# Every converted weight block written to DRAM in the first chunk, and a higher transfer rate in the planner

## The chip, the cores and the metric

The kernel runs on one core of a Trainium2 chip. The metric is the device time of one execution in microseconds; several executions were timed and the median is given. Six streams of instructions matter here: TensorE (PE, with its weight loads as PEld), VectorE (DVE), ScalarE (ACT), GpSimd (POOL), and SyncE (SP), which issues the DMAs.

## What is computed

Linear attention with random features over 4 batches, 8 heads, 576 tokens and a head size of 64, and then two gated feed-forward layers over the 2304 tokens (512 channels, 1536 hidden). The weights of the two layers come in as 64-bit floats.

```python
def phi(x):
    proj = np.einsum('bhsd,md->bhsm', x, omega)
    h = proj - np.sum(x * x, axis=-1, keepdims=True) / 2.0
    h = h - np.max(h, axis=-1, keepdims=True)
    return np.exp(h) / np.sqrt(m)
q_p, k_p = (phi(q_s), phi(k_s))
kv = np.einsum('bhsm,bhsd->bhmd', k_p, v)
num = np.einsum('bhsm,bhmd->bhsd', q_p, kv)
den = np.einsum('bhsm,bhm->bhs', q_p, np.sum(k_p, axis=2))[..., None] + 1e-06
x = num / den                        # then tokens x 512
g = x @ w_gate
x = (g / (1 + np.exp(-g)) * (x @ w_val)) @ w_out      # layer 0
x = ((x @ w_a) * (x @ w_b)) @ w_out2                  # layer 1
```

## The kernel before

The 2304 tokens are worked in five chunks: two of 512, one of 256, and two of 512 that run together as a pair. Each chunk passes through attention and both layers; the attention of a later chunk runs between the layer matmuls of the one before it. Every matmul of a layer is done as three: each operand is split into a rounded part and a remainder (`wh` and `wl` for weights, `xh`/`xl` and `hh`/`hl` for activations), and L908, L909 and L910 add up high by high, high by low and low by high. `product` (L966) does the same for the pair.

A layer has 36 weight blocks of 128 x 512, so the two have 72. A block that is converted goes through five steps: a DMA of 512 KB into one of four raw buffers (`w64a`, three of them, or `w64b`, L865); two ACT instructions that bring exponent and mantissa into place (L868 into a buffer `w`, L871 in the raw buffer); two DVE instructions that join sign and halves (L874, L877); then the split, ACT for `wh` (L889) and DVE for `wl` (L458). `w` is a ring of four buffers (`w32`), `wh` and `wl` have seven each. `weights` decides with `keep` in which chunk the converted `w` is also written to DRAM (`kept`, L883, 256 KB): blocks of even number in chunk 0, blocks of odd number in chunk 1. A later chunk loads the kept block (L887, 256 KB, and L1028 in the pair) and only splits it. An odd block is therefore converted twice. A buffer `w` comes free when its split is done and its store, where it has one, has landed.

No order is written out by hand. Every operation is recorded with a due time, and `Plan.order` plays the program through with costs of its own: an engine takes, of what is ready by its account, the operation that is due first. The instructions of each engine are then issued in that order, and on the chip each engine keeps to it. For a DMA the planner has one pipe that moves `RATE` MiB in a microsecond; a higher `RATE` makes data ready earlier in its account and lets operations stand earlier in the order.

The features of the later chunks (`features` with `STACKED`) run through a short chain: PE projects into one of two PSUM buffers `ps_p` (L561), ACT copies half of it to `kf` or `qf` (L569), DVE adds the other half (L572), which frees `ps_p` for PE's next L561.

Of the kernel before, what the change touches and what calls it, by code (L numbers as in the profile page):

```python
# [88 lines left out]
class Plan:  # L89
# [11 lines left out]
    SIGNAL = 0.12  # L101
    START = 0.7
    TABLE = 1.4
    RATE = 0.24
    HELD = {DVE: (1.0, 0.05), POOL: (1.0, 0.12)}

    def __init__(self):
# [27 lines left out]
    def order(self):  # L135
# [36 lines left out]
        while True:  # L172
# [51 lines left out]
            if o.size:  # L224
                pipe = max(pipe, t + 1.0) + o.size / self.RATE
                o.end = pipe + 1.2
# [28 lines left out]
def attention_moe_moe(ctx: ExitStack, tc: tile.TileContext, qT, kT, q, k, v, omegaT,  # L255
# [596 lines left out]
    def weights(c, m, i, due):  # L852
# [2 lines left out]
        ahead = AHEAD if c else 0.0  # L855
        parts_of[c, m, i] = (hi, lo)
        w = r_w32.buf()
        keep = i % 2
        if c <= keep:


# [425 lines left out]
```

## Time and profile before

| | |
|---|---|
| median of 3 runs | 1015.7 us (1015.49 to 1016.5) |
| profiled execution | 1016.63 us, of which the span is 1014.8 us |
| PE busy | 994.4 us, 98% of the span |
| DVE busy | 880.8 us, 87% |
| ACT busy | 731.1 us, 72% |
| DMA | 153.12 MB, 151 GB/s on average, about 240 GB/s in the first 300 us |
| granted TensorE clock | 1.00 throughout |

The span is what the profiler saw from the first to the last instruction; about 1.8 us of the execution's time lie around it. PE is busy nearly all the time and the clock is full, so the places to look at are the few microseconds in which PE stands, and what it waits for there. By the stretches of the trace, chunk 0 runs to about 283 us, chunk 1 to about 550 us, and chunk 2 and the pair fill the rest.

### The profile page before, as it was taken

The page shows a single profiled execution, that of the slowest core. Times are in us where ns is not written, and L with a number is a line of the kernel's source. Part 1 is how long each engine was busy: PE and PEld are TensorE (multiplying, and loading weights), DVE is VectorE, ACT ScalarE, POOL GpSimd, SP SyncE. Part 2 cuts the span into 40 slices and gives each one's busy share as a digit, 9 for nine tenths or more (in the row PEclk, how much of TensorE's full clock was granted, in tenths as well). Part 3 has the DMA queues.
Part 4 walks back from the last instruction along what each step waited for, and adds up shares of the span by engine and source line. Part 5 has one row for each costly group of instructions (what it writes and reads, how often), then busy time and mean ns, then how long its engine had stood idle before and what let it go on. Part 6 is the DMA issues. An engine that isn't in the chain of part 4 may idle for free.

```text
span 1014.8 us, 15549 instructions
## 1 busy us (share of the span) xinstructions
PE 994.4 (98%) x5212; PEld 836.8 (82%) x5212; DVE 880.8 (87%) x1697; ACT 731.1 (72%) x1519; POOL 228.3 (22%) x178
## 2 busy tenths in 40 slices
PE   7999999999999999999999999999999999999998
PEld 6878888888888878777778999988888887888886
DVE  5999889999858889999996989799899788989972
ACT  5987988898779998978788988576574645556340
POOL 1232011111204242346544324311020021202000
PEclk9999999999999999999999999999999999999999
DMA  7777787776854657735654555521212211121212
GB/s 248 238 260 237 217 247 238 248 237 218 279 187 133 182 176 236 225 113 176 196 170 130 158 155 163 175 80 42 74 42 63 84 32 52 30 75 42 63 32 83
DMA packets 92399, 153.12 MB, mean 151 GB/s; under 512 B 8736, under 2 KB 41120, under 8 KB 92320
## 3 DMA queue, kind: packets, MB, share of 16 engines
q1 hardware_dynamic: 92240, 152.11, 48.9%
q8 instruction: 41, 0.67, 0.3%
q14 instruction: 38, 0.31, 0.1%
q10 hardware_dynamic: 80, 0.03, 0.0%
HBM read 128.52 MB, written 23.59 MB: 150 GB/s over the span
## 4 chain that ended last, share of the span: by engine, by line
PE 73%; DVE 11%; ACT 7%; DMA 4%; issue 3%; POOL 1%; SPq 0%; DVEq 0%; ACTq 0%; POOLq 0%
PE ps_m L966 13%; PE ps_m L908 9%; PE ps_m L910 9%; PE ps_m L909 9%; PE ps_p L966 8%; PE ps_t L966 8%; PE ps_kv L966 4%; PE ps_kv L640 2%; DVE wl L458 2%; DMA w64a<-w 2%; PE ps_p L586 2%; PE ps_t L735 1%; PE ps_p L561 1%; DVE w64a L874 1%; DVE w L877 1%
## 5 line engine op out<-in xcount | busy, mean ns | idle before, releaser
L458 DVE TENSOR_TENSOR wl<-w,wh 128x512 fp32r<-128x512 f32 x256 | 194.4, 769 | 23.6 <-ACT wh L889 22.9
L908 PE MATMUL ps_m<-xh,wh 128*128 128x512 f32 (+1 forms) x500 | 188.8, 378 | 2.1 <-ACT a L926 1.4
L909 PE MATMUL ps_m<-xl,wh 128*128 128x512 f32 (+1 forms) x500 | 183.4, 367 | 0.2 <-DVE xl L458 0.2
L910 PE MATMUL ps_m<-xh,wl 128*128 128x512 f32 (+1 forms) x500 | 183.2, 366 | 0.1
L889 ACT ACTIVATE wh<-w 128x512 fp32r<-128x512 f32 x224 | 137.8, 631 | 25.5 <-DVE w L877 10.0
L458 POOL TENSOR_TENSOR rs<-xT,rs 64x576 fp32r<-64x576 f32 (+4 forms) x48 | 67.8, 1413 | 232.8 <-ACT rs L546 112.3
L908 PEld LDWEIGHTS ps_m<-xh,wh 128*128 128x128 f32 x500 | 94.8, 190 | 17.6 <-issue 2.4
L910 PEld LDWEIGHTS ps_m<-xh,wl 128*128 128x128 f32 x500 | 94.3, 189 | 16.3 <-DVE wl L458 0.5
L909 PEld LDWEIGHTS ps_m<-xl,wh 128*128 128x128 f32 x500 | 94.6, 189 | 11.2 <-DVE xl L458 0.8
L908 PE MATMUL ps_m<-hh,wh 128*128 128x512 f32 (+1 forms) x252 | 94.8, 376 | 0.0
L910 PE MATMUL ps_m<-hh,wl 128*128 128x512 f32 (+1 forms) x252 | 92.2, 366 | 0.2 <-DVE wl L458 0.2
L909 PE MATMUL ps_m<-hl,wh 128*128 128x512 f32 (+1 forms) x252 | 92.2, 366 | 0.0
L871 ACT ACTIVATE w64a<-w64a 128x512 uint32<-128x512 uint32 x90 | 60.6, 680 | 17.7 <-DMA w64a<-w 17.4
L877 DVE SCALAR_TENSOR_TENSOR w<-w,w64a 128x512 uint32<-128x512 uint32 x90 | 67.0, 749 | 2.8 <-ACT w L868 2.5
L874 DVE SCALAR_TENSOR_TENSOR w64a<-w64a 128x512 uint32<-128x512 uint32 x90 | 64.6, 726 | 3.1 <-ACT w64a L871 3.1
L868 ACT ACTIVATE w<-w64a 128x512 f32<-128x512 f32 x90 | 60.1, 672 | 0.0
L910 PEld LDWEIGHTS ps_m<-hh,wl 128*128 128x128 f32 x252 | 47.6, 189 | 8.7 <-DVE wl L458 0.7
L458 DVE TENSOR_TENSOR hl<-h,hh 128x512 fp32r<-128x512 f32 (+1 forms) x72 | 50.6, 704 | 2.9 <-ACT hh L932 2.2
L908 PEld LDWEIGHTS ps_m<-hh,wh 128*128 128x128 f32 x252 | 47.7, 189 | 6.1
L909 PEld LDWEIGHTS ps_m<-hl,wh 128*128 128x128 f32 x252 | 47.7, 189 | 5.2
L932 ACT ACTIVATE hh<-h 128x512 fp32r<-128x512 f32 (+1 forms) x72 | 40.1, 558 | 14.9 <-DVE h L929 14.7
L929 DVE TENSOR_TENSOR h<-a,ps_m 128x512 f32<-128x512 f32 (+1 forms) x63 | 38.8, 615 | 12.7 <-PE ps_m L910 8.8
(822 smaller groups left out, 2635.4 us busy)
## 6 DMA issues: line engine op xcount, KB each, us to landing
w64a<-w SPq DMA_DIRECT2D x90, 512.0 KB, 4.5
w<-kept SPq DMA_DIRECT2D x180, 256.0 KB, 2.7
kept<-w SPq DMA_DIRECT2D x72, 256.0 KB, 5.0
w64b<-w SPq DMA_DIRECT2D x18, 512.0 KB, 4.8
kt<-k_t SPq DMA_DIRECT2D x16, 320.0 KB, 3.8
vt<-v_t SPq DMA_DIRECT2D x16, 320.0 KB, 4.8
xT<-kT SPq DMA_DIRECT2D x16, 288.0 KB, 3.2
qt<-q_t SPq DMA_DIRECT2D x16, 256.0 KB, 3.4
```

The lines of the kernel that those rows point to most:

```text
L458: eng.tensor_tensor(out=out, in0=a, in1=hi.bitcast(F32), op=ALU.subtract)
L868: on(ACT, act(CW + 50), due - ahead - 10, lambda: nc.scalar.activation(out=w.tile, in_=raw.tile[:, :, 1].bitcast(F32), func=AF.Abs, scale= ...
L871: on(ACT, act(CW + 50), due - ahead - 10, lambda: nc.scalar.activation(out=raw.tile[:, :, 0], in_=raw.tile[:, :, 0], func=AF.Copy, scale=0 ...
L874: on(DVE, dve(CW, True), due - ahead - 9, lambda: nc.vector.scalar_tensor_tensor(out=raw.tile[:, :, 0], in0=raw.tile[:, :, 1], scalar=0x80 ...
L877: on(DVE, dve(CW, True), due - ahead - 9, lambda: nc.vector.scalar_tensor_tensor(out=w.tile.bitcast(U32), in0=w.tile.bitcast(U32), scalar= ...
L889: on(ACT, act(CW), due - ahead - 7, lambda: nc.scalar.activation(out=hi.tile.rearrange("p a c -> p (a c)"), in_=w.tile, func=AF.Copy), rea ...
L908: nc.tensor.matmul(o, lhsT=hi.tile[:, wi], rhs=a, start=first, stop=False)
L909: nc.tensor.matmul(o, lhsT=hi.tile[:, wi], rhs=b, start=False, stop=False)
L910: nc.tensor.matmul(o, lhsT=lo.tile[:, wi], rhs=a, start=False, stop=last)
L929: on(DVE, dve(n), due, lambda a=a, h=h, ps=ps: nc.vector.tensor_tensor(out=h.tile[:, 0:n], in0=a.tile[:, 0:n], in1=ps[1].tile[:, 0:n], op= ...
L932: on(ACT, act(n), due + 2, lambda h=h, hh=hh: nc.scalar.activation(out=hh.tile[:, 0:n], in_=h.tile[:, 0:n], func=AF.Copy), reads=[(h,)], w ...
L966: nc.tensor.matmul(ps.tile, lhsT=flat(a.tile)[:, k], rhs=b.tile, start=first and i == j == 0, stop=last and i == len(w) - 1 and j == 2, sk ...
```

## The change

Two lines. `keep` becomes 0 for every block: all 72 blocks are converted once, in chunk 0, and written to DRAM there; chunk 1 loads all of its blocks from `kept`. And the planner's `RATE` goes from 0.24 to 0.28 MiB/us.

```diff
-    RATE = 0.24
+    RATE = 0.28
...
         w = r_w32.buf()
-        keep = i % 2
+        keep = 0
         if c <= keep:
```

In the built program L865, L868, L871, L874 and L877 stand 72 times each where they stood 108 times; L887 stands 152 times where it stood 116 times; L883 stands 72 times in both. PE has the same instructions in another order.

SP's queue in the middle of layer 0 of chunk 0, before (`w64a` and `w64b` are loads of a raw block, `kept_18` is the store of block 18, and the number behind `w_` is the buffer):

```order
L865 DMA w64a_170<-w 128x1024
L865 DMA w64b_171<-w 128x1024
L883 DMA kept_18_203<-w_174 128x512
L865 DMA w64a_169<-w 128x1024
L883 DMA kept_20_204<-w_172 128x512
L865 DMA w64a_168<-w 128x1024
L865 DMA w64b_171<-w 128x1024
L865 DMA w64a_170<-w 128x1024
```

The same place in the changed program:

```order
L865 DMA w64a_169<-w 128x1024
L865 DMA w64a_170<-w 128x1024
L883 DMA kept_17_211<-w_173 128x512
L883 DMA kept_18_212<-w_174 128x512
L865 DMA w64b_171<-w 128x1024
L865 DMA w64a_168<-w 128x1024
L883 DMA kept_19_213<-w_175 128x512
L883 DMA kept_20_214<-w_172 128x512
```

Loads and stores now come two by two, and every one of the four `w` buffers carries a store.

DVE in layer 1 of chunk 1, ahead of the two L572 that the trace of before has at 485.5 us, before (`wl` is a block's remainder, `hl` that of an activation; `mx`, `top`, `bias`, `nsq` and `s` are small steps of the features):

```order
L874 SCALAR_TENSOR_TENSOR w64a_169<-w64a_169 128x512
L599 SCALAR_TENSOR_TENSOR top_102<-mx_98,nsq_94 128x2
L458 TENSOR_TENSOR wl_186<-w_174,wh_179 128x512
L603 TENSOR_TENSOR bias_106<-nsq_94,top_102 128x2
L458 TENSOR_TENSOR wl_187<-w_172,wh_180 128x512
L877 SCALAR_TENSOR_TENSOR w_175<-w_175,w64a_169 128x512
L458 TENSOR_TENSOR hl_164<-h_141,hh_152 128x512
L530 TENSOR_SCALAR nsq_92<-s_89 128x10
L530 TENSOR_SCALAR nsq_94<-s_90 128x8
L527 TENSOR_REDUCE s_89<-qt_114 128x8
L572 TENSOR_TENSOR qf_115<-qf_115,ps_p_64 128x256
L572 TENSOR_TENSOR qf_115<-qf_115,ps_p_65 128x256
```

The same place in the changed program:

```order
L458 TENSOR_TENSOR wl_189<-w_175,wh_182 128x512
L596 TENSOR_REDUCE mx_98<-kf_82 128x2
L458 TENSOR_TENSOR hl_164<-h_141,hh_152 128x512
L599 SCALAR_TENSOR_TENSOR top_102<-mx_98,nsq_94 128x2
L603 TENSOR_TENSOR bias_106<-nsq_94,top_102 128x2
L530 TENSOR_SCALAR nsq_94<-s_90 128x8
L527 TENSOR_REDUCE s_90<-qt_114 128x8
L572 TENSOR_TENSOR qf_115<-qf_115,ps_p_64 128x256
L572 TENSOR_TENSOR qf_115<-qf_115,ps_p_65 128x256
```

Between the remainder `hl_164` and the two L572 the order is nearly the same; the two conversion steps and two of the `wl` that stood ahead of it are gone or stand elsewhere.

## Rows read from the trace of the kernel before

**Rows 1.** Waits of PE, whole span: who waited, for whom, us, times, longest.
```profile
PE ps_m L586 <- DMA xT<-kT: 4.6, 1, 4.6
PE ps_p L561 <- DVE kf L572: 3.0, 5, 1.1
PE ps_p L561 <- DVE qf L572: 2.4, 2, 1.3
```

**Rows 2.** Busy time by stretch: us, engines (x instructions), granted clock, DMA share, GB/s.
```profile
0.00:60.00 60.00, 52.13 (x305) 43.26 (x306) 46.25 (x135) 44.90 (x123) 13.50 (x21) 1.00 0.79 246
60.00:130.00 70.00, 69.91 (x321) 58.00 (x320) 64.23 (x104) 57.54 (x104) 10.25 (x6) 1.00 0.77 236
130.00:283.00 153.00, 152.75 (x812) 129.85 (x811) 141.65 (x290) 124.32 (x262) 24.10 (x17) 1.00 0.77 242
...
350.00:550.00 200.00, 193.58 (x1023) 157.01 (x1022) 177.74 (x361) 169.49 (x394) 91.83 (x74) 1.00 0.58 179
550.00:1014.80 464.80, 459.04 (x2425) 393.19 (x2423) 400.92 (x716) 273.32 (x522) 73.58 (x48) 1.00 0.28 81
```

**Rows 3.** PE in time, 483.9 to 486.5 us: start, us, instruction, idle before.
```profile
485.96 0.39 PE L561 MATMUL ps_p<-oms,rs 128*128 128x256 f32 x1 [1.30 <-DVE qf L572]
```

**Rows 4.** DVE in time, 481 to 486 us.
```profile
483.28 0.68 DVE L877 SCALAR_TENSOR_TENSOR w<-w,w64a 128x512 uint32<-128x512 uint32 x1
...
484.74 0.69 DVE L527 TENSOR_REDUCE s<-qt 128x8 f32<-128x512 f32 x1
485.48 0.75 DVE L572 TENSOR_TENSOR qf<-qf,ps_p 128x256 f32<-128x256 f32 x2
```

**Rows 5.** Costliest groups, page: shapes, count, busy us, mean ns, idle before.
```profile
L871 ACT ACTIVATE w64a<-w64a 128x512 uint32<-128x512 uint32 x90 | 60.6, 680 | 17.7 <-DMA w64a<-w 17.4
L877 DVE SCALAR_TENSOR_TENSOR w<-w,w64a 128x512 uint32<-128x512 uint32 x90 | 67.0, 749 | 2.8 <-ACT w L868 2.5
L874 DVE SCALAR_TENSOR_TENSOR w64a<-w64a 128x512 uint32<-128x512 uint32 x90 | 64.6, 726 | 3.1 <-ACT w64a L871 3.1
L868 ACT ACTIVATE w<-w64a 128x512 f32<-128x512 f32 x90 | 60.1, 672 | 0.0
```

**Rows 6.** DMA issues, whole span: count, KB each, median us to landing.
```profile
w<-kept SPq DMA_DIRECT2D x180, 256.0 KB, 2.7
kept<-w SPq DMA_DIRECT2D x72, 256.0 KB, 5.0
```

**Rows 7.** DMA traffic and issues from 60 to 130 us.
```profile
DMA packets 7886, 16.55 MB, mean 236 GB/s; under 512 B 631, under 2 KB 3463, under 8 KB 7880
...
w64a<-w SPq DMA_DIRECT2D x17, 512.0 KB, 4.5
kept<-w SPq DMA_DIRECT2D x11, 256.0 KB, 5.2
w64b<-w SPq DMA_DIRECT2D x5, 512.0 KB, 4.6
```

**Rows 8.** Busy time by stretch again, for two stretches with dense traffic.
```profile
135.00:145.00 10.00, 10.00 (x53) 8.51 (x53) 7.78 (x16) 6.39 (x16) 1.32 (x1) 1.00 0.99 310
...
250.00:275.00 25.00, 25.00 (x134) 21.18 (x133) 21.61 (x41) 19.19 (x41) 7.17 (x5) 1.00 0.87 265
```

**Rows 9.** SP's queue in time, 255 to 295 us.
```profile
258.67 0.32 SPq L887 DMA_DIRECT2D w<-kept  x1
...
285.86 0.34 SPq L956 DMA_DIRECT2D outT<-h  x1
```

**Rows 10.** Engines in time, 100.3 to 103 us: one block from conversion to store.
```profile
100.50 0.67 ACT L868 ACTIVATE w<-w64a 128x512 f32<-128x512 f32 x1
...
102.49 0.43 SPq L883 DMA_DIRECT2D kept<-w  x1
```

**Rows 11.** All transfers of kept blocks: shortest, median and longest time to landing.
```profile
DMA to landing us min/median/max: 2.3/2.9/9.0
```

**Rows 12.** Waits of all engines, whole span: ACT for the raw blocks.
```profile
ACT w64a L871 <- DMA w64a<-w: 17.4, 11, 4.1
```

## The prediction, made before the changed kernel ran

> **What bounds the kernel now.** I read the busy shares first: PE 98% of the span at the full clock, DVE 87%, ACT 72%. Then the table of stretches [rows 2], where one subtraction per row gives PE's idle time: 7.9 us in the first 60 us, 0.1 from 60 to 130, 0.2 from 130 to 283, 6.4 from 350 to 550, and 5.8 in the last 465 us. The amount of PE's work does not change, so the change can only move these idle times, or make new ones where there are none now. The list of PE's waits [rows 1] says what they are: at the start one wait of 4.6 us for the first keys, which comes ahead of all weights, and then seven waits of L561, 5.4 us together, for DVE's L572 to free `ps_p`. All seven lie in the second chunk, in the stretch of the 6.4 us. Read one of them in time: PE stands 1.30 us before the L561 at 485.96 [rows 3], because DVE reaches L572 only at 485.48, with a conversion step (L877) and a reduction among the work just ahead of it [rows 4]. DVE is 89% busy there [rows 2]; a step that comes due finds a queue in front of it.
>
> In the first chunk the picture is turned round. PE hardly stands there, but DVE is busy 92 to 93%, ACT 81 to 82%, and the DMA engines 77% at 236 to 242 GB/s [rows 2]. It is fed just in time by four resources at once.
>
> **What the change removes.** 36 conversions in the second chunk. On DVE 36 x (0.749 + 0.726) = 53.1 us, on ACT 36 x (0.672 + 0.680) = 48.7 us [rows 5]. Spread over the 267 us from 283 to 550 that is 0.20 us in every us of DVE: the 89% of the stretch becomes about 69%, and ACT's 85% about 67%. Neither engine is the bound, so the 53 us themselves are worth nothing; what they are worth is the queue ahead of L572. Bounds: nothing, if the planner packs other steps into the gaps and L572 is late again; 6.4 us if all idle time of the stretch goes. At the place shown in the order, two conversion steps and two remainders stood ahead of the L572 that cost 1.30 us, and in the changed program L527 and four small steps are still there. I take 4.5 us, seven tenths of the stretch: the waits of L561 are 5.4 of the 6.4, and most of them are shorter than two conversion steps (1.3 us is the longest, 1.48 us two steps). What would be late next is ACT, whose L569 feeds L572; it is relieved as much.
>
> **What it adds, first the traffic.** The 36 odd blocks are stored in the first chunk: 36 x 256 KB = 9.4 MB more there. In the second chunk 36 loads of 512 KB become 256 KB and 36 stores vanish, 18.9 MB less, at a share of 0.58 that hinders nobody now. The tight place is 60 to 130 us: 22 loads of blocks and 11 stores, 16.55 MB [rows 7]. With 11 more stores (2.9 MB) it is 19.4 MB, 278 GB/s over the same 70 us. Can the engines carry that? The densest 10 us carried 310 GB/s at a share of 0.99, and the densest 25 us 265 GB/s at 0.87 [rows 8]. At 310 the 19.4 MB take 63 us, and nothing is lost; at 265 they take 73.3 us, 3.3 us more than now, all of it on PE, which has no reserve here. 265 is no ceiling, since the share was 0.87, but 310 was held only for 10 us. I take the middle, 1.5 us. From 130 to 283 the stores add as much per us, but here the first load for the second chunk is issued at 258.67 while the first chunk's last output leaves at 285.86 [rows 9]: a lead of 27 us, or some 6.5 MB at 242 GB/s, covers the 5 to 6 MB of stores. I cost it at nothing; without the lead it would be 5.5 MB at 265 GB/s, up to 6 us more where PE waits for blocks. At the start three odd stores (0.8 MB, 3 us of transfer at 265 GB/s) fall between the loads of the first blocks and of the attention: nothing to 3 us, below nothing by 1 if the new order suits the start better; I take 0.5, since the wait that dominates there [rows 1] comes before any store.
>
> The Trainium skill, "DMA: Bandwidth & Descriptors", section Specifications, gives some 358 GB/s as what HBM allows a core, by which the 19.4 MB would take 54 us and the 1.5 us would be zero. The trace doesn't carry this: share 0.77 at 236 GB/s, and 0.99 at 310, both point to a little over 300 GB/s for these transfers [rows 2, 8].
>
> **Then the waits.** Every buffer `w` of the first chunk now also waits for its store. The nearest row: L868 fills one at 100.50, its store is issued at 102.49 [rows 10], and lands 5.2 us later (median of the stretch) [rows 7], so a buffer is held for 7.2 us. Four buffers at one block per 70/22 = 3.2 us leave 12.7 us. With the longest landing seen, 9.0 us [rows 11], it would be 11.0 us: still inside. So I cost the ring at nothing; it decides from a landing of 10.7 us on. The new wait sits on L868, at the head of ACT's queue: behind it stand the evacuations L926 and L932, without which PE's `ps_m` buffers don't come free. SP's queue is moved too: stores stand two by two, each behind the load that the same conversion releases, so no load is held up by them for long; each store adds its 0.43 us of issue [rows 10] on a queue that mostly waits.
>
> By the Trainium skill, same page, section "Anatomy of one DMA", the end of a DMA is reported only once its last byte is confirmed in the target, and HBM is the slowest target. The rows agree: 5.0 us for a store against 2.7 for a load of the same 256 KB [rows 6].
>
> **The rate.** 0.28 MiB/us is 294 GB/s. It costs nothing by itself; it decides how early in the order conversions stand. In the order of the changed program they do stand earlier against PE's work in the first chunk, by about two blocks for much of layer 0, which gives some cover for late transfers. In the later chunks the instructions are the same and their order differs in detail; PE's idle time there (5.8 us) may change by 1 us either way, and I count zero.
>
> **The sum.** -4.5 + 1.5 + 0.5 = -2.5 us on the span of 1014.8 us. The profiled execution took 1016.63 us, 0.9 above the median of 1015.7; against the median the forecast is 1013.2 us.
>
> **The rivals.**
>
> *Same.* The relief is real but L572 is late for another reason: the planner, too, sees the free DVE and sets PE's L561 earlier, so that PE meets the chain as tightly as before. Two of the 6.4 us go, and the first chunk costs 2. For it: L572 comes after L569 on ACT, and PE's order is fixed by a plan that fills gaps. Against it: the wait in [rows 3] has conversion steps directly in its queue. It gives 1015.7.
>
> *Slower.* L868 waits for stores. If traffic at 90% and more makes stores land above 10.7 us, ACT stands at L868 with the evacuations behind it. The nearest row for such a wait is ACT's L871 waiting for its load, 17.4 us in all, in 11 waits among its 108 runs [rows 12], so about 1.6 us each. If it strikes one in six of the 36 newly stored blocks, 6 x 1.6 = 9.6 us on ACT, nearly all on PE between 60 and 130 us, where there is no lead: say 8. With -4.5 and +2 that is +5.5, or 1021.2 us. For it: four resources are tight at the same time. Against it: the ring has 12.7 us and needs 7.2.
>
> *Much faster.* All 6.4 us go, with the matmuls' restart after each wait (about 0.15 us for each of seven) another 1.0, and the first chunk carries the stores for nothing: 1008.3 us. The clock is full in every stretch, so nothing can come from there.
>
> *It doesn't do what it says*: excluded by the counts, 72 conversions instead of 108.
>
> **How the numbers follow.** Forecast (1010 to 1014.5) 0.40, much faster 0.04, same 0.25, slower 0.31. A difference under 0.2% (2 us) can't be told from none. The forecast's upper end reaches into that band, and the same-case's spread to both sides: faster 0.41, same 0.27, slower 0.32. Cases of both signs hold much; the likeliest one's own range is 1010 to 1014.5. The range of all: the low end leaves out half of the much faster case, 1008.5; the high end takes in the slower case and a little more, 1022.
>
> **What would show it.** Right: L561's waits for L572 fall from 5.4 us to under 2; DVE from 350 to 550 us falls to about 140 us; from 60 to 130 us the traffic is near 275 GB/s with PE idle 1 to 2 us. Wrong: PE idle by 5 us or more before 283 us; ACT waiting at L868 for stores, or at L871 for loads, much above 17 us; stores that land at 8 us in the median; or L561 waiting as long as before, with ACT's L569 named.

## The result, and the profile after

| | before | after |
|---|---|---|
| median | 1016.1 us (4 runs) | 1022.4 us (1021.8 to 1022.9, 4 runs) |
| ratio | | 1.0066, interval 1.0054 to 1.0077 |
| span of the profiled execution | 1014.8 us | 1020.3 us |
| PE busy | 994.4 us | 998.9 us |
| DVE / ACT busy | 880.8 / 731.1 us | 840.7 / 693.0 us |
| DMA | 153.12 MB | 143.69 MB |
| granted clock, mean | 1.000 | 0.993 |

The kernel became slower by 0.66%. 9 MB of traffic and about 40 us each of DVE's and ACT's work are gone, and the time went up. The stretches of the changed kernel, in the columns of [rows 2] (PE, PEld, DVE, ACT, POOL busy, clock, DMA share, GB/s):

```profile
0.00:60.00 60.00, 51.55 (x299) 43.24 (x300) 47.55 (x136) 46.78 (x125) 12.61 (x21) 0.96 0.85 267
60.00:130.00 70.00, 70.00 (x315) 58.19 (x314) 63.10 (x102) 51.00 (x91) 10.32 (x7) 0.99 0.85 265
130.00:283.00 153.00, 150.45 (x784) 127.69 (x784) 134.97 (x270) 121.31 (x258) 22.19 (x17) 0.99 0.83 263
350.00:550.00 200.00, 198.02 (x1045) 161.37 (x1044) 155.42 (x312) 145.59 (x348) 87.57 (x75) 1.00 0.41 118
550.00:1020.30 470.30, 462.05 (x2435) 395.98 (x2433) 397.80 (x719) 277.90 (x528) 70.12 (x48) 1.00 0.28 81
```

The same subtraction as before the change: PE stands 8.5 us to 60 us (7.9 before), 0.0 to 130 (0.1), 2.6 to 283 (0.2), 2.0 from 350 to 550 (6.4), and 8.3 from 550 on (5.8). The second chunk gives back 4.4 us, as forecast. Idle time is not the whole of it: the trace draws a matmul of 512 columns as 0.39 us long where the next starts after 0.23 us, so a shorter wait does not show, and a matmul at a lower clock counts as busy. An estimate of the rest: price every matmul at the median time to the next one that its kind has in the kernel before. By that count PE is 1.4 us of work behind the kernel before at 60 us, 1.7 at 130, 6.3 at 283, 1.3 at 550 and 6.1 at 660 us. So the second chunk gives back about 5 us, and two stretches, 130 to 283 and 550 to 660 us, take between 4 and 5 us each. What eats the gain lies at three places, and PE's list of waits (us, times, longest), which answers to [rows 1], names them:

```profile
PE ps_m L908 <- ACT a L926: 2.7, 2, 1.8
PE ps_m L908 <- ACT xh L680: 2.4, 2, 1.7
PE ps_t L769 <- DVE xt L760: 1.7, 3, 0.7
PE ps_p L561 <- DVE kf L572: 1.5, 4, 0.6
```

L561 has fallen from 5.4 to 1.5 us. New are four waits between 52 and 57 us at the start of layer 0 (0.45 to 0.69 us each, L769, L908, L909), one of 1.67 us near 166 us, and three between 569 and 576 us (0.93, 0.59 and 1.77 us). Behind each group PE works at half clock for some microseconds. The same columns for three short stretches:

```profile
56.00:62.00 6.00, 5.51 (x13) 4.06 (x13) 4.61 (x8) 4.99 (x8) 2.86 (x2) 0.50 0.96 300
168.00:172.00 4.00, 4.00 (x17) 3.58 (x16) 3.77 (x9) 3.32 (x7) 0.00 (x0) 0.59 0.91 293
576.00:580.00 4.00, 3.91 (x23) 3.91 (x24) 3.73 (x9) 2.97 (x8) 1.53 (x2) 0.69 0.47 131
```

A granted clock of 0.50 is 1.2 GHz in place of 2.4. This is why PE's busy time rose with the same matmuls. (The Trainium skill, "TensorE: Matmul & The Clock Gate", section "HAM oscillation — how this bites in real kernels", describes a PE that pauses between groups of matmuls for its data and starts the next group at the lower clock. The trace agrees in kind: 0.50 from 56 to 62 us, behind the four waits of 0.45 to 0.69 us.)

How the wait near 166 us comes about is read from ACT and PE in time (start, duration, instruction, idle before it):

```profile
157.55 0.68 ACT L871 ACTIVATE w64b<-w64b 128x512 uint32<-128x512 uint32 x1 [1.44 <-DMA w64b<-w]
...
160.34 0.68 ACT L871 ACTIVATE w64a<-w64a 128x512 uint32<-128x512 uint32 x1 [0.54 <-DMA w64a<-w]
...
163.27 0.68 ACT L871 ACTIVATE w64a<-w64a 128x512 uint32<-128x512 uint32 x1 [1.18 <-DMA w64a<-w]
164.91 1.14 ACT L608 ACTIVATE kf<-ps_p,bias 128x128 f32<-128x128 f32 x4 [0.97 <-DVE bias L603]
165.93 0.61 ACT L680 ACTIVATE xh<-ps_m 128x512 fp32r<-128x512 f32 x1
...
166.59 0.50 PE L908 MATMUL ps_m<-xh,wh 128*128 128x512 f32 x1 [1.67 <-ACT xh L680]
```

ACT keeps to its order. Three times within 7 us it stands at L871 for a raw block that has not landed, 3.2 us in all, and L680, which PE needs, stands behind. The last 0.97 us ahead of L608 are a wait for DVE's L603; DVE had itself stood for the same L871:

```profile
158.26 0.69 DVE L874 SCALAR_TENSOR_TENSOR w64b<-w64b 128x512 uint32<-128x512 uint32 x1 [0.70 <-ACT w64b L871]
...
161.06 0.69 DVE L874 SCALAR_TENSOR_TENSOR w64a<-w64a 128x512 uint32<-128x512 uint32 x1 [0.49 <-ACT w64a L871]
```

PE does not wait for weights here: it waits for an activation that is queued behind a weight. Over the whole span ACT's waits at L871 grew from 18.6 us (17.4 for `w64a` [rows 12] and 1.2 for `w64b`) to 29.2 (us, times, longest):

```profile
ACT w64a L871 <- DMA w64a<-w: 15.8, 19, 2.0
ACT w64b L871 <- DMA w64b<-w: 13.4, 8, 2.2
```

and the blocks land later, here from 60 to 130 us (KB each, median us from issue to landing; 4.5, 5.2 and 4.6 before [rows 7]):

```profile
DMA packets 9731, 18.58 MB, mean 265 GB/s; under 512 B 783, under 2 KB 4239, under 8 KB 9725
...
w64a<-w SPq DMA_DIRECT2D x15, 512.0 KB, 5.6
kept<-w SPq DMA_DIRECT2D x21, 256.0 KB, 6.1
w64b<-w SPq DMA_DIRECT2D x5, 512.0 KB, 5.2
```

### The profile page after: what moved, and what is told of

Same layout as the page of the kernel before. It is cut to its first block, busy times and chain, and to the rows that moved or that the text cites. A ratio compares the mean times of both kernels' runs of the same rounds, so it can differ in the third digit from the quotient of the medians.

```text
span 1020.3 us, 15486 instructions
## 1 busy us (share of the span) xinstructions
PE 998.9 (98%) x5212; PEld 841.9 (83%) x5212; DVE 840.7 (82%) x1625; ACT 693.0 (68%) x1445; POOL 214.9 (21%) x178
## 2 busy tenths in 40 slices
DMA packets 92399, 143.69 MB, mean 141 GB/s; under 512 B 8736, under 2 KB 41120, under 8 KB 92320
## 4 chain that ended last, share of the span: by engine, by line
PE 54%; ACT 2%; DVE 1%; issue 0%; ACTq 0%
PE ps_m L966 13%; PE ps_p L966 8%; PE ps_t L966 8%; PE ps_m L908 4%; PE ps_m L909 4%; PE ps_m L910 4%; PE ps_kv L966 4%; PE ps_p L561 1%; PE ps_t L841 1%; PE ps_kv L908 1%; PE ps_kv L910 1%; PE ps_kv L909 1%; PE ps_t L827 1%; PE ps_kv L640 1%; PE ps_p L910 0%; PE ps_p L909 0%
## 5 line engine op out<-in xcount | busy, mean ns | idle before, releaser
L908 PE MATMUL ps_m<-xh,wh 128*128 128x512 f32 (+1 forms) x504 | 191.3, 380 | 5.1 <-ACT a L926 2.7
L909 PE MATMUL ps_m<-xl,wh 128*128 128x512 f32 (+1 forms) x504 | 186.3, 370 | 0.7 <-DVE xl L458 0.7
L910 PE MATMUL ps_m<-xh,wl 128*128 128x512 f32 (+1 forms) x504 | 186.0, 369 | 0.0
L458 POOL TENSOR_TENSOR rs<-xT,rs 64x576 fp32r<-64x576 f32 (+4 forms) x48 | 64.0, 1333 | 257.0 <-ACT rs L546 128.4
L908 PEld LDWEIGHTS ps_m<-xh,wh 128*128 128x128 f32 x504 | 96.9, 192 | 21.2 <-ACT a L926 3.1
L910 PEld LDWEIGHTS ps_m<-xh,wl 128*128 128x128 f32 x504 | 96.5, 191 | 16.0
L909 PEld LDWEIGHTS ps_m<-xl,wh 128*128 128x128 f32 x504 | 96.8, 192 | 12.8 <-DVE xl L458 1.5
L908 PE MATMUL ps_m<-hh,wh 128*128 128x512 f32 (+1 forms) x240 | 89.8, 374 | 0.0
L909 PE MATMUL ps_m<-hl,wh 128*128 128x512 f32 (+1 forms) x240 | 87.5, 365 | 0.0
L910 PE MATMUL ps_m<-hh,wl 128*128 128x512 f32 (+1 forms) x240 | 87.3, 364 | 0.0
L910 PEld LDWEIGHTS ps_m<-hh,wl 128*128 128x128 f32 x240 | 45.3, 189 | 7.4
L908 PEld LDWEIGHTS ps_m<-hh,wh 128*128 128x128 f32 x240 | 45.5, 189 | 5.6 <-issue 0.2
L909 PEld LDWEIGHTS ps_m<-hl,wh 128*128 128x128 f32 x240 | 45.5, 189 | 4.8
L640 PEld LDWEIGHTS ps_kv<-vt,kf 112*128 112x128 f32 (+1 forms) x320 | 44.7, 194 | 5.1 <-ACT kf L608 1.4
L640 PE MATMUL ps_kv<-vt,kf 112*128 112x129 f32 (+1 forms) x320 | 47.1, 280 | 0.7 <-ACT kf L608 0.7
L871 ACT ACTIVATE w64a<-w64a 128x512 uint32<-128x512 uint32 x54 | 36.5, 677 | 15.9 <-DMA w64a<-w 15.8
L926 ACT ACTIVATE a<-ps_m 128x512 f32<-128x512 f32 (+1 forms) x68 | 36.0, 531 | 11.9 <-PE ps_m L910 11.4
```

What stands on the lines that cost most here:

```text
L458: eng.tensor_tensor(out=out, in0=a, in1=hi.bitcast(F32), op=ALU.subtract)
L640: nc.tensor.matmul(kv.tile[:, (P + 1) * h:(P + 1) * (h + 1)], lhsT=f.tile[0:r, t, h], rhs=vt.tile[0:r, t], start=(t == 0 and h == 0), stop ...
L871: on(ACT, act(CW + 50), due - ahead - 10, lambda: nc.scalar.activation(out=raw.tile[:, :, 0], in_=raw.tile[:, :, 0], func=AF.Copy, scale=0 ...
L908: nc.tensor.matmul(o, lhsT=hi.tile[:, wi], rhs=a, start=first, stop=False)
L909: nc.tensor.matmul(o, lhsT=hi.tile[:, wi], rhs=b, start=False, stop=False)
L910: nc.tensor.matmul(o, lhsT=lo.tile[:, wi], rhs=a, start=False, stop=last)
```

## The experiments

First theory: the added stores cost what the second chunk gives back, since the traffic makes the raw blocks late. Rival: the traffic is bearable, and the new order of the instructions, by the rate and by the planner's new view of stores and conversions, loses the time. The medians of all runs, each with the ratio to runs of the kernel before on the same chip:

| run | what it is | median, us | ratio |
|---|---|---|---|
| odd_r28 | RATE 0.28 alone | 1020.1 | 1.0035 [1.0024, 1.0046] |
| keep0_r24 | all stored in chunk 0, RATE 0.24 | 1026.6 | 1.0101 [1.0086, 1.0116] |
| nostore | the changed kernel without the 36 odd stores | 1016.6 | 1.0001 [0.9991, 1.0010] |
| fill | the changed kernel, 14 filler matmuls | 1021.3 | 1.0042 [1.0028, 1.0057] |
| s0_r24 | as keep0_r24, odd stores hidden from the planner | 1021.4 | 1.0049 [1.0033, 1.0065] |
| mix1_r24 | RATE 0.24, all of layer 1 stored in chunk 0 | 1025.8 | 1.0097 [1.0078, 1.0116] |
| mix0_r24 | RATE 0.24, all of layer 0 stored in chunk 0 | 1029.7 | 1.0129 [1.0107, 1.0152] |
| ord_stores | order of before, 36 stores more | 1017.0 | 1.0015 [1.0003, 1.0027] |
| ord_load | order of before, the full change | **1007.6** | 0.9917 [0.9905, 0.9930] |
| ord_copy | the same, one ACT copy per block left | 1010.0 | 0.9936 [0.9923, 0.9949] |
| r26_load | full change on the order of RATE 0.26 | 1014.7 | 0.9985 [0.9971, 0.9999] |
| r28_load | full change on the order of odd_r28 | 1020.8 | 1.0046 [1.0029, 1.0063] |
| late5 | the changed kernel, L868 planned later | 1030.7 | 1.0147 [1.0131, 1.0164] |
| late7 | the same, later still | 1058.2 | 1.0414 [1.0392, 1.0436] |
| wait1 | the changed kernel, L871 planned 1 us later | 1018.1 | 1.0030 [1.0017, 1.0042] |
| wait2 | the same, 2 us | 1016.2 | 1.0005 [0.9995, 1.0015] |

### The two lines one at a time

odd_r28 takes the new rate alone:

```diff
-    RATE = 0.24
+    RATE = 0.28
```

> The kernel before with the planner's rate at 0.28: only the order is changed, odd blocks are converted twice as before. Traffic theory: no 36 more stores, so nothing is lost: 1015 to 1017 us, clock 1.00. Order theory: stalls of 1.5 us and more with a fallen clock appear as in the changed kernel, while the second chunk gains nothing: 1019 to 1025 us.

It costs 4.3 us, with the traffic of before. Its start, and ACT's waits from 20 to 283 us (9.0 and 1.2 in the kernel before for the same two rows of that stretch):

```profile
0.00:60.00 60.00, 50.49 (x292) 42.41 (x292) 44.05 (x134) 44.17 (x123) 11.09 (x19) 0.97 0.80 249
```
```profile
ACT w64a L871 <- DMA w64a<-w: 23.1, 20, 2.1
ACT w64b L871 <- DMA w64b<-w: 6.3, 7, 2.2
```

The 29.4 us at L871 are there without a single store more. So the step "It costs nothing by itself" fell first. The profiled execution is the slowest of this kernel's eight (1023.0 us). From 550 to 660 us its PE stands 0.65 us, as before; the stall of the changed kernel near 570 us is not in it.

keep0_r24 takes the other line:

```diff
-        keep = i % 2
+        keep = 0
```

> The change with the planner's rate left at 0.24: only the place of the stores is changed. Traffic theory (36 more stores make the first chunk's transfers late, ACT waits at L871 for raw blocks, PE stands and its clock falls): the bytes are the same, so ACT's waits at L871 stay near 29 us and PE is idle 2 us or more between 130 and 283 us; 1018 to 1025 us. Order theory (the new rate sets conversions and evacuations in an order that the chip doesn't keep up with): the order is that of a slower pipe, no stall above 1.5 us after the first 60 us, the granted clock stays at 1.00, and the second chunk keeps its gain of 4.3 us of PE idle: 1011 to 1014 us.

It is slower than both lines together, and above the ranges of both theories. Its stretch from 60 to 130 us, and PE's waits in it:

```profile
60.00:130.00 70.00, 62.83 (x273) 50.47 (x272) 59.78 (x95) 60.49 (x100) 10.52 (x8) 0.95 0.76 239
```
```profile
PE ps_m L908 <- ACT wh L889: 5.2, 2, 4.6
PE ps_m L910 <- DVE wl L458: 1.9, 2, 1.3
```

Here PE does wait for weights: 7.2 us idle, although the DMA engines carry no more than before (239 GB/s). At 0.24 MiB/us the planner, told of all stores, takes the transfers for full and puts the conversions late (s0_r24 below tests this). Two orders, two opposite faults.

### The stores' price in the changed kernel's own order

nostore keeps every instruction's place and leaves the 36 added stores out; later loads of an odd block take its even neighbour, so this kernel's weights are not the reference's.

```diff
-                on(SP, dma(256), due - 5, lambda: nc.sync.dma_start(out=d.tile, in_=w.tile),
+                on(SP, dma(256), due - 5, (lambda: None) if i % 2 else
+                   lambda: nc.sync.dma_start(out=d.tile, in_=w.tile),
```

> The changed kernel with its order untouched, but the 36 stores of odd blocks are left out, and later chunks load the even neighbour's block in their place (the product is then another). Traffic theory: landing of raw blocks in the first chunk goes back from 5.6 to about 4.5 us, ACT's waits at L871 from 29 us to under 19 us, the stall of 1.67 us at 165 us and the fall of the clock behind it go, and perhaps the one at 55 us; the one at 574 us stays. 1016 to 1019 us. Order theory: all three stalls stay, 1021 to 1023 us.

5.8 us less than the changed kernel, with ACT's waits at L871 from 20 to 283 us at 11.4 us in place of 29.2. From 130 to 283 us PE's idle time is gone (153.00 of 153.00 us busy), and the wait near 166 us with it; the stalls at 52 to 57 and 569 to 576 us stay, 5.8 us earlier the second. PE runs the same list of matmuls in both kernels, so the same matmul can be timed in both. The one that starts at 132.01 us in the changed kernel starts at 131.93 here; the L908 of 166.59 us is this L910 (the edit moves the line numbers by two), without a wait and with the full clock behind it:

```profile
163.53 0.39 PE L910 MATMUL ps_m<-xh,wh 128*128 128x512 f32 x1
```

The matmul of 175.18 us starts at 169.94. Between 132 and 175 us, and next to nothing ahead of that, the stores take 5.2 us: 1.0 near 134, 2.0 in the wait near 166, and 2.2 behind it, at the lower clock. Taken alone this run speaks for the first theory; it holds for this one order.

### What the clock costs

fill keeps the order and issues 14 matmuls with zeros into an open sum, at the stalls near 55 and 166 us, so that PE does not stand there.

```diff
+                def zeros(k):
+                    for _ in range(k):
+                        nc.tensor.matmul(o, lhsT=bdh.tile[0:D, M:2 * M], rhs=ready.tile[0:D, 0:n],
+                                         start=False, stop=False)
```

> The changed kernel with 14 matmuls of zero weights put where PE stands near 55 us (7) and near 165 us (7); each adds zero to the accumulating bank, the rest of the order is untouched. Clock theory (most of what was lost there is not the standing itself but matmuls at half clock after it): the waits end when they ended before, but the granted clock stays at 1.00 from 50 to 175 us, where the changed kernel ran some 6.3 and 3.3 us at 1.2 GHz; that returns about 3.0 and 1.6 us, 1017.5 to 1018.5 us. Rival (the clock falls for another reason, or falls all the same): 1022 to 1024 us.

The same short stretches as above, now:

```profile
56.00:62.00 6.00, 4.63 (x18) 3.02 (x19) 5.05 (x8) 5.25 (x9) 2.87 (x2) 1.00 0.98 308
...
168.00:172.00 4.00, 3.86 (x23) 3.37 (x23) 3.87 (x10) 3.42 (x7) 0.00 (x0) 1.00 0.85 243
...
576.00:580.00 4.00, 4.00 (x34) 4.00 (x35) 3.73 (x10) 3.41 (x8) 1.73 (x2) 1.00 0.52 135
```

The clock is full throughout and the time falls by 1.1 us only (by the two ratios 2.4, and their intervals touch). Timed by the same matmul, even that does not come from the two places that were filled. PE is 1.31 us ahead at 60 us and 0.78 at 172 us, but runs into what is behind, with new waits of 1.37 us ahead of 60.48 and 1.55 us ahead of 134.23 us; at 283 us it is 0.14 us late, at 568 us 0.19 ahead. While ACT and DVE feed PE just in time, the half clock is time that would have been spent waiting. The third stretch, where nothing was filled, kept its three waits (0.93, 0.59 and 1.77 us) and yet its clock, and there the gain arises: 1.68 us ahead at 600 us, of which 1.14 are left at the end. So half the clock did cost 1.5 us at this place. Why it did not fall is open; it differs between executions of one kernel, too: of nostore's ten, six show a mean clock of 0.995 and take 1016.4 to 1017.3 us, four 0.998 and 1014.6 to 1015.4.

### Half the stores, and stores that the planner doesn't see

s0_r24 is keep0_r24 with the odd stores priced at nothing in the plan; mix1_r24 and mix0_r24 store the odd blocks of one layer only in chunk 0, at RATE 0.24.

```diff
-                on(SP, dma(256), due - 5, lambda: nc.sync.dma_start(out=d.tile, in_=w.tile),
+                on(SP, dma(0 if i % 2 else 256), due - 5, lambda: nc.sync.dma_start(out=d.tile, in_=w.tile),
```
```diff
-        keep = i % 2
+        keep = 0 if m else i % 2      # mix1_r24
+        keep = i % 2 if m else 0      # mix0_r24
```

> All blocks are stored in the first chunk, RATE is 0.24, and the stores of the odd blocks cost the planner nothing, so that its order is that of the kernel before up to about 90 us; on the chip the stores are all there. Two theories of the 7.2 us in which PE stood from 60 to 130 us in the kernel with all stores at RATE 0.24. The plan: at 0.24 MiB/us the planner takes the DMA for the bound and puts PE's work where it then has to wait; then here PE is idle there under 2 us, from 130 to 283 us 1 to 3 us, and the total is 1012 to 1017 us. The transfers: the engines can't bring the blocks in time whatever the order; then PE is again idle 5 us or more from 60 to 130 us and the total is 1020 us or more. Both: no fall of the clock ahead of 62 us, as in the kernel before, and from 350 to 550 us an idle time of 1.5 to 2.5 us.

> RATE 0.24; all blocks of layer 1 are stored in the first chunk, but of layer 0 only the even ones, as in the kernel before. Its order is word for word that of the kernel before through layer 0 of the first chunk. 18 stores (4.7 MB) are added from 130 to 283 us and none ahead of it; 18 conversions go from the second half of the second chunk. If the added stores cost by the traffic of the stretch alone, PE is idle 1 to 2.5 us from 130 to 283 us (0.25 in the kernel before), and the second chunk gives back some 2 us: 1014 to 1017 us. If the lead of 27 us covers the stores, as the prediction had it, 130 to 283 us stays at 0.3 us and the total is 1013 to 1014 us. The stretches ahead of 130 us stay as before, with the clock at 1.00, by both.

> The reverse of the run before: RATE 0.24; all blocks of layer 0 are stored in the first chunk, of layer 1 only the even ones. 18 stores are added ahead of 130 us, where the traffic was 236 GB/s at 0.77 and PE had no wait. If the planner's view of the transfers sets the loss, the order is that of the kernel with all stores at RATE 0.24 up to 130 us: PE idle about 7 us from 60 to 130 us, some 2 us back in the first half of the second chunk, 1019 to 1023 us. If the loss is in layer 1's share of the stores, 60 to 130 us stays under 1.5 us and the total is 1013 to 1016 us.

s0_r24 has all stores on the chip and PE idle 0.1 us from 60 to 130 us at 263 GB/s: the 7.2 us of keep0_r24 were the plan's. But its total, 1021.4, is that of the other theory; it has new stalls elsewhere: 3.3 us from 550 to 660 us, and as much at the change of chunks, where ACT's first splits stand at loads that the planner believed there (ACT, 270 to 300 us; us, times, longest), with 2.4 us of PE behind them:

```profile
ACT wh L889 <- DMA w<-kept: 10.5, 3, 5.4
```

mix1_r24 missed both of its totals: 130 to 283 us is as clean as before (0.25 us idle with 257 GB/s), and the loss is behind it. PE from 283 to 550 us, which had 5.4 us of L561's waits before:

```profile
PE ps_p L561 <- DVE kf L572: 8.0, 8, 1.9
```

Seven of these eight waits lie between 287 and 391 us, in layer 0, whose odd blocks this kernel still converts there (ACT's last L868 is at 397 us); behind it, where the conversions are gone, one of 1.93 us is left. So the relief works where it is given, and the new plan made the rest tighter. mix0_r24 has 7.6 us idle from 60 to 130 us, as keep0_r24 has 7.2 and as its planner theory expected, and is slower still than that theory's range. In s0_r24 and mix1_r24 the bill comes at places that the planner arranged anew, and not where the traffic was added; in mix0_r24 it comes where the stores were added, but at 239 GB/s.

One stall is common to all eleven kernels whose plan has fewer conversions, at either rate (2.9 to 4.0 us idle), and is in none of the seven whose plan has all 108 (1.2 at most). From 550 to 660 us, before, then odd_r28, keep0_r24 and the changed kernel:

```profile
550.00:660.00 110.00, 109.35 (x889) 105.25 (x888) 96.12 (x181) 87.65 (x190) 37.17 (x24) 1.00 0.54 160
```
```profile
550.00:660.00 110.00, 109.35 (x887) 104.39 (x886) 98.45 (x183) 91.68 (x195) 33.82 (x26) 1.00 0.54 160
```
```profile
550.00:660.00 110.00, 107.10 (x853) 102.52 (x852) 91.90 (x175) 91.55 (x191) 32.94 (x24) 0.98 0.52 154
```
```profile
550.00:660.00 110.00, 106.45 (x848) 101.86 (x847) 94.05 (x178) 90.55 (x192) 33.16 (x24) 0.98 0.52 155
```

PE stands 0.65 us in the first two, 2.9 in the third and 3.55 in the last. So this part of the loss goes with the first line of the change in the plan and not with the rate.

### The order held fixed

So the order was taken out of the comparison: the plan is that of the kernel before. The traces show the same list on PE and POOL, and on ACT and DVE but for the instructions left out. ord_stores adds the 36 stores; SP issues each where ACT starts the block's split. ord_load also drops the second chunk's conversions and loads the kept block where L868 stood; ord_copy loads it earlier into the raw buffer and lets ACT copy it.

```diff
+        def split():
+            nc.scalar.activation(
+                out=hi.tile.rearrange("p a c -> p (a c)"), in_=w.tile, func=AF.Copy)
+            if extra:                                   # c == 0 and i % 2
+                nc.sync.dma_start(out=extra.tile, in_=w.tile)
...
+            def bring():                                # ord_load, at L868
+                if not again:                           # again: c == 1
+                    nc.scalar.activation(
+                        out=w.tile, in_=raw.tile[:, :, 1].bitcast(F32), func=AF.Abs, scale=2.0 ** -112)
+                else:
+                    nc.sync.dma_start(out=w.tile, in_=kept[m, i].tile)
```

> The kernel before, its order on every engine word for word, with nothing changed but 36 stores more in the first chunk: the odd blocks, each issued by SP where ACT starts the split of the block. The second chunk still converts. If the stores' traffic itself sets the loss, as the run of the changed kernel without them says (5.8 us): PE idle 2 to 4 us more ahead of 283 us, ACT's waits at L871 near 29 us against 18.6, total 1019 to 1022 us. If the loss comes from the order that the planner makes for the stores and the rate, and an order with slack takes the traffic: PE idle ahead of 283 us within 1 us of before, total 1016 to 1017.5 us.

> The same with the second chunk relieved: the order of the kernel before, the 36 stores more in the first chunk, and in the second chunk the odd blocks are no longer converted; SP loads the kept block into its buffer where ACT's L868 stood, and L868, L871, L874, L877 and the store are left out there. The relief worth -4.4 us in the changed kernel must show here without any new order: waits of L561 in the second chunk from 5.4 to under 2 us. With the stores' cost at 0 to 1 us: 1011.5 to 1013.5 us, faster than both; with the stores' cost at 4 to 6 us: 1015 to 1018 us. The block is asked for only some 3 us before its split, so L889 may wait for it in ACT's queue: that would take part of the gain, up to 2 us.

> As the run before, but the kept block is loaded into the raw buffer at the place of the raw block's load, and ACT copies it from there (one ACTIVATE at L868's place); L871, L874, L877 and the store are left out in the second chunk. DVE is relieved as in the run before, ACT by half. If lateness of the load hurts the run before, this one is faster by up to 2 us; if ACT's relief is what frees L572, it is slower by 1 to 2 us. With the stores' cost at 0 to 1 us: 1011.5 to 1014 us; at 4 to 6 us: 1016 to 1018 us.

ord_stores, 60 to 130 and 130 to 283 us:

```profile
60.00:130.00 70.00, 70.00 (x323) 58.41 (x322) 64.59 (x104) 57.88 (x104) 8.76 (x6) 1.00 0.87 278
130.00:283.00 153.00, 151.58 (x804) 128.12 (x803) 139.43 (x287) 122.02 (x260) 22.45 (x17) 1.00 0.86 276
```

The prediction's 19.4 MB at 278 GB/s are there (19.43 MB), and PE does not stand for a moment; from 130 to 283 us it stands 1.2 us more than before. Timed by the same matmul, PE is level with the kernel before up to 262 us (0.1 us ahead) and 1.8 late at 283. Most of that, 1.3 us, arises behind one wait of ACT from 272 us on, with L718, which PE needs, queued behind it:

```profile
275.41 0.66 ACT L868 ACTIVATE w<-w64a 128x512 f32<-128x512 f32 x1 [3.42 <-DMA kept<-w]
```

This is the wait of the prediction's slower rival, L868 for a store, once and at the change of chunks. The second chunk takes up 1.4 of the 1.8 us; in the median 36 stores cost 1.0 us. ord_load:

```profile
60.00:130.00 70.00, 70.00 (x323) 58.41 (x323) 64.54 (x104) 57.77 (x104) 8.04 (x7) 1.00 0.90 278
130.00:283.00 153.00, 152.70 (x812) 129.77 (x811) 136.75 (x281) 118.46 (x252) 23.20 (x17) 1.00 0.81 264
350.00:550.00 200.00, 198.87 (x1083) 164.05 (x1082) 150.57 (x321) 150.15 (x360) 86.21 (x75) 1.00 0.40 124
```
```profile
PE ps_p L561 <- DVE qf L572: 0.6, 1, 0.6
```

8.3 us faster than before and 14.7 faster than the changed kernel, with the same stores, loads and conversions as the latter, and 4 us better than expected, since the relief was put at the -4.4 of the changed kernel. The last row is all that is left of L561's 5.4 us. From ord_stores to ord_load the time falls by 9.3 us, on the profiled spans by 8.8: 4.9 of it is PE's idle time (1014.5 - 993.8 = 20.7 against 1005.7 - 989.9 = 15.8) and 3.9 its busy time. Not all of it is the relief: 1.9 of the 8.8 us arise between 262 and 283 us, most of them at the wait of L868 above, which ord_load does not have. Against the kernel before, the same matmul starts 0.3 us earlier at 320 us and 8.4 earlier at 550, so the relief is worth 8.1 us in the second chunk. ord_copy is 2.3 us slower than ord_load, and below its range, too. Of the 3.0 us between the two traces 1.0 lies ahead of 262 us, where nothing is relieved yet, so that ACT's share in the relief is worth more than an earlier load is likely, but not shown by more than some 2 us.

The rival has it for this order: on the order of before the added traffic costs 1 us and the relief gives 8 to 9, so the changed kernel loses by its new plan. The first theory was not wrong on the new plan: there the stores do cost 5 us.

### Which property of the order

r28_load and r26_load put the same full change on the orders of RATE 0.28 and 0.26 (still planned with 108 conversions).

> The full change on another order: the order of the kernel that differs from the one before by RATE 0.28 alone (1020.1 us), with the 36 stores more and the second chunk relieved, both in the instructions only and not in the plan. If the relief (-9.3 us between the runs with and without it on the order of 0.24) and the stores (+1.0) are properties of the work and the order adds its own part (+4.2 for 0.28), the total is 1011 to 1013 us. If the stores hurt an order of 0.28 as they hurt the changed kernel (5.8 us), it is 1015 to 1018 us: then it is the higher rate that takes away what room the stores need. If it is 1020 us or more, the relief needs the order of 0.24.

> The same with the order that the planner makes at RATE 0.26, still told of 108 conversions and 36 stores in each of two chunks. If the order of 0.24 is good by what it knows of the transfers, 0.26 lies between the two: 1008 to 1012 us. If each new order draws its stalls at the places where it differs (start, 275 to 290 us, 560 to 580 us) with no trend in the rate, anything from 1007 to 1016 us. Both: waits of L561 in the second chunk under 2 us.

1014.7 and 1020.8 against 1007.6 at 0.24: slower with each step of the rate, though 0.26 lies above the 1012 that a plain trend was given, so three orders are a weak proof of a rule. On the order of 0.28 the full change is worth nothing against odd_r28. PE's list is the same in these two as well: the matmul of 136.11 us in odd_r28 starts 1.05 us earlier in r28_load, that of 175.06 us 4.56 later, and that of 550.10 us 2.16 earlier. So here the stores take 5.6 us between 136 and 175 us, where they took 5.2 in the changed kernel and nothing on the order of 0.24, and the second chunk gives as much back. ACT from 20 to 283 us in r28_load, whose L882 is the L871 of the others:

```profile
ACT w64a L882 <- DMA w64a<-w: 23.0, 23, 3.6
ACT w64b L882 <- DMA w64b<-w: 7.5, 9, 1.4
```

30.5 us, and 14.5 in ord_load with the same traffic. A planner that believes in 0.28 MiB/us lets L871 stand closer behind its load than the load is on the chip. The sum of these waits alone does not set the time: ord_stores has 20.4 us of them at 1017.0 and r26_load 25.8 at 1014.7; it matters what stands behind.

late5 and late7 were to move the conversions away from their loads, by the one constant that the plan has for that:

```diff
-    EARLY, LATE = 26.0, 3.0
+    EARLY, LATE = 26.0, 5.0      # 7.0 in late7
```

> The changed kernel (RATE 0.28, all blocks stored in the first chunk) with one number of the plan more: LATE, the time that the planner lets pass between a raw block's landing by its account and its L868, is 5 us in place of 3. If conversions that stand too close behind their loads in ACT's queue are what a rate of 0.28 costs, ACT's waits at L871 from 20 to 283 us fall from 29 us to under 20, the wait of L908 for L680 near 166 us goes below 0.7 us, and the total falls to 1012 to 1018 us. If the waits at L871 are only a sign of dense traffic, they stay at 25 to 32 us and the total at 1019 to 1024 us.

> The same with LATE at 7 us. By the first theory the waits at L871 fall further, under 12 us, but the splits now come late for PE, as in the kernel with all stores at RATE 0.24: PE waits for L889 and L458 of the weights (none in the changed kernel, 8.3 us there), so the total is not below the run at 5 us: 1014 to 1022 us. By the second theory both stay as in the changed kernel.

Both missed, and told nothing of the theory: LATE delays L868, but ACT reaches a block with L871 first, and the waits there stayed (24.1 and 30.1 us). What they did show is the other fault, raw buffers held too long: PE waits for weights from 20 to 283 us in late7,

```profile
PE ps_m L908 <- ACT wh L889: 8.9, 9, 2.2
PE ps_m L910 <- DVE wl L458: 5.6, 11, 1.2
```

while the traffic from 60 to 130 us falls to 213 GB/s. wait1 and wait2 move the right instruction:

```diff
-                bias=0.49), reads=[], writes=[(raw, 0)])
+                bias=0.49), reads=[], writes=[(raw, 0)], late=2.0)      # 1.0 in wait1
```

> The two runs with a later L868 left the wrong instruction alone: ACT reaches a block first with L871, which has no such time in the plan, and there the waits stayed (24 and 30 us), while a later L868 holds the raw buffers longer. Here the changed kernel has its LATE of 3 us again, and L871 alone is taken by the planner 1 us after the landing by its account. If L871 too close behind its load is what 0.28 costs, ACT's waits at L871 from 20 to 283 us fall from 29 to some 15 to 20 us and the total to 1014 to 1019 us. If it is a matter of each order, with no rule in this distance, the waits may fall but the total is anywhere from 1017 to 1027 us.

> The same with 2 us. By the first theory the waits at L871 fall to 8 to 14 us and the total is 1012 to 1018 us, unless the raw buffers are held so much longer that loads come late: then the traffic from 60 to 130 us falls below 255 GB/s and PE waits for weights (L889, L458) by over 2 us, with 1018 to 1026 us.

ACT's waits at L871 from 20 to 283 us, first in wait1, then in wait2:

```profile
ACT w64a L871 <- DMA w64a<-w: 6.7, 6, 1.7
...
ACT w64b L871 <- DMA w64b<-w: 0.9, 1, 0.9
```
```profile
ACT w64a L871 <- DMA w64a<-w: 1.0, 2, 0.8
```

and the stretches of wait2:

```profile
60.00:130.00 70.00, 70.00 (x308) 57.99 (x307) 64.75 (x105) 54.39 (x97) 10.25 (x7) 0.97 0.88 279
130.00:283.00 153.00, 153.00 (x823) 130.92 (x822) 137.05 (x277) 121.27 (x256) 21.91 (x17) 1.00 0.83 261
```

29.2, 7.6, 1.0 us of waits give 1022.4, 1018.1, 1016.2 us. The traffic is denser than in the changed kernel (279 against 265 GB/s from 60 to 130 us), and PE no longer stands from 130 to 283 us. By the count of PE's work wait2 is 2.5 us behind the kernel before at 283 us, where the changed kernel is 6.3. So 6.2 us come back with L871 planned later, 3.8 of them ahead of 283 us. Both totals lie within the first theory's ranges (1018.1 in its rival's as well); the waits fell further than it expected. One reservation: the plan is made anew, and other instructions moved too (some 1000 of ACT's 1415 keep their sequence). What points at L871 is that most of the gain comes where its waits were, as in nostore, which kept the order. The 8.6 us from wait2 to ord_load are other marks of the new order: the start (9.6 against 9.1 us idle, and the clock at 0.97 in the first two stretches, 1.00 in ord_load) and 550 to 660 us (3.45 against 0.67 us idle), where ACT changes between the tables of L608 and L926, 1.28 us each time, just when PE needs L926. Both stalls are in nostore and wait2 alike. By the count of PE's work 3.7 of the 8.6 us have arisen by 130 us and 3.2 arise from 550 to 660 us; no run took them out singly.

## Why the prediction was wrong

It said 1013.2 us, faster; the kernel takes 1022.4, 0.4 beyond the range.

- **The second chunk, -4.5: right.** L561's waits fell from 5.4 to 1.5 us and the stretch's idle time by 4.4. On the old order the same relief is worth 8.1 us: the idle time of 350 to 550 us falls from 6.4 to 1.1, and some 3 us more come from where the trace shows no wait. The "much faster" rival's 1008.3 is close to what ord_load took (1007.6), but on the changed kernel's own order the stores were not for nothing (its restart of 0.15 us behind a wait is 0.10 in the rows: 0.22 us to the next matmul, 485.96 to 486.18, in place of 0.12). One sign failed: DVE from 350 to 550 us fell to 155.4 us and not to about 140. The 53.1 us are a sum of durations, and neighbouring steps overlap (L877 starts at 483.28 and takes 0.68 us, the next step starts at 483.88); DVE's busy time fell by 40.1 in all.
- **The start, +0.5: near in size, wrong in kind.** PE stands 0.6 us more than before to 60 us, but without the stores PE reaches 132 us no earlier than with them (0.08 us): it is the order's, not the stores'.
- **The traffic from 60 to 130 us, +1.5: too high, harmless.** 19.4 MB at 278 GB/s came as worked out on the old order and cost PE nothing; in the changed kernel it was 18.58 MB at 265 GB/s, and PE did not stand there either. The lower bound, 310 GB/s and no loss, was the right end.
- **130 to 283 us, nothing: right on the old order but for the one wait at its end, wrong on the new one.** The stores take nothing there in ord_load, 1.9 us at the change of chunks in ord_stores, 5.2 between 132 and 175 us in the changed kernel and 5.6 at the same place in r28_load. A lead at the end of a stretch does not help a queue that stands at a load in its middle.
- **The rate, "It costs nothing by itself": the step that failed.** The prediction saw that conversions move earlier and took that for cover. Earlier against PE's work means closer behind the load in ACT's queue, and PE waits for what is queued behind. Alone the rate costs 4.3 us; with the full change, 1020.8 on its order against 1007.6 on the order of 0.24. In the changed kernel it shows as the 5.2 us that the stores take: the same stores take nothing there on the order of 0.24, and 6.2 us come back in the plan with L871 2 us later.
- **The later chunks, "I count zero": the second step that failed.** The stalls from 569 to 576 us are 2.9 us of idle time more than before, and by the count of PE's work nearly 5 us. They go with the plan for fewer conversions and not with the rate: 0.65 us in odd_r28, 2.9 in keep0_r24.
- **The clock** was a term for gains only ("nothing can come from there"). It fell three times behind new waits. Filling the first two gave 0.2 us by 568 us; where the third did not fall, 1.5.
- **The slower rival, 1021.2:** right in size and in its kind, ACT standing for a DMA with the evacuations behind it, wrong in place. L868 never waited for a store in the changed kernel (once in ord_stores, 3.4 us); the neighbour that it used for its price, L871, was the place, and its sign "L871 for loads much above 17 us" came true at 29. The rate had not been read as an instruction to stand nearer to the loads; that reading is what this rival lacked to be the likeliest.

## What to carry to other kernels

Where a planner sets the order, a constant of its cost model is an edit to every queue: cost it by which instruction will now stand at the head of an in-order queue before its data is there, and who is queued behind it. To judge a change of work under such a planner, first hold the old order and change only the instructions; here that alone told the gain of the change (-8.3 us) from the loss by its new plan (+14.7). Where two kernels issue the same list on an engine, time the same instruction in both traces: the place where they part is the place of the loss. An optimistic transfer rate and a pessimistic one fail in opposite ways, activations behind late loads or weights behind late conversions, and PE's list of waits tells which.

## What the runs showed of the hardware

- The first chunk's traffic of 512 KB loads and 256 KB stores ran at 278 to 279 GB/s for 70 us at a share of 0.87 to 0.90 without delaying PE; the landing of a raw block (`w64a`) grew from 4.5 to 5.1 us (median) by that in ord_load, on the order of before.
- PE's clock fell to 0.50 after groups of waits as short as 0.45 to 0.69 us, while single waits of 1.30 us in the kernel before, and the same group of waits near 570 us in fill, left it at 1.00. The wait of 1.67 us near 166 us was followed by 0.59 on average from 168 to 172 us.
- A PE at half clock for some microseconds cost next to nothing where its feeders had no lead: 0.2 us were left at 568 us when the first two falls were filled. Near 576 us it cost 1.5 us.
